# Third weight group issued ahead of the casts of the first, w_out's first third in two loads, leftover tokens of batches 0 and 1 joined to batch 2

## The chip, the cores and the metric

One core of one Trainium2 chip. The metric is the device time of one launch in microseconds (us); the median of several runs is quoted. The profile is one execution, and its span is some 2 us shorter than the time. TensorE (PE) does the matmuls, VectorE (DVE), ScalarE (ACT) and GpSimd (POOL) the rest; GpSimd also issues most loads.

## The reference, cut to what matters

```python
# attention without softmax: batch 8, heads 8, seq 576, head_dim 64
kv  = einsum('bhsd,bhse->bhde', k, v)
out = einsum('bhsd,bhde->bhse', q, kv)
x   = out / sqrt(mean(out*out, -1) + 1e-6) * g_norm       # then [4608 tokens, 512]
# gated feed-forward: d_model 512, d_ff 1536
ffn = (gelu(x @ w_gate) * (x @ w_val)) @ w_out
return x + sigmoid(x @ w_res) * ffn
```

Each batch has 576 tokens: 512 go into a block of the feed-forward, and the 64 left over of two batches make one tile of 128 for a ninth block at the end.

## The kernel before

The kernel is one long schedule. Blocks 0 to 7 hold 512 tokens each; while TensorE works on block n, the attention of batch n+1 is threaded in between. Only batch 0 has nothing to hide behind: its attention and the first matmuls of block 0 are an "opening", whose order on all engines is a list of words, read from left to right. A word is a piece of work on a pair of heads (digit), with the engine as the last letter where there is a choice: `vc3D` casts v of pair 3 on VectorE, `o2` multiplies q by kv, `sq`/`rd` square and reduce, `t2` scales, `xT2`/`xo2` transpose x and evict it, `g2`/`v2` are the matmuls with w_gate and w_val, `wcg0P`/`wcv0P` cast the first weight group on GpSimd, `w2` issues the loads of the third weight group.

```python
opening = """
... rt1 rd0 kc3A kvo2 qT3 w1 ri1 o2 rt0 t1 warm1 sq2 vc3D
rd2 qo3A xT1 kv3 wcg0P rt2 kvo3 ri0 ri2 warm2 o3 t2 xo1A wcg1P sq3a wcv0P sq3b xT2 t0 wcv1P rd3a xo2A g1
xT0 rd3b w2 v1 xo0D rt3 g2 gelu ri3 v2 t3a g0 t3b xT3a xT3b xo3aA xo3bD v0 w3 g3a v3a g3b v3b
"""
elif name == "w":              # 512 columns of w_gate, then of w_val, cast to fp16 by the DMA
    load_wg(pr)
    load_wv(pr)
...
# after the opening: w_res, batch 1, then w_out in thirds, all in the queue that GpSimd feeds
nc.gpsimd.dma_start(out=wr16, ...)
load_batch(1)
for f in range(0, NF, 4):
    load_wo(f, f + 4)
...
# leftover tokens of batches 0 and 1, threaded into block 1 on their own
at(1, 2, lambda: a_rem_qT(b))                  # 4 transposes on TensorE, 2 copies on ScalarE
at(1, 3, lambda: a_rem_o(b))                   # 8 matmuls
at(1, 8, lambda: a_norm(b, NJ, NJ + 1), t[NJ]) # 12 small VectorE instructions on 8 columns
at(1, NF + 1, x[NJ], lambda: a_x(b, NJ))       # 4 transposes on TensorE
...
pmoe  = ...tile_pool(name="pmoe",  bufs=4, space=PSUM)   # idle, o1, o0, then g and v tiles
pattn = ...tile_pool(name="pattn", bufs=4, space=PSUM)
```

Of the kernel before, what the change touches and what calls it, by code (L numbers as in the profile page):

```python
# [9 lines left out]
FP16 = mybir.dt.float16  # L10
# [8 lines left out]
def kernel(  # L19
# [15 lines left out]
    nc = tc.nc  # L35
# [6 lines left out]
    NJ = 4  # L42
# [80 lines left out]
    def load_wg(i):  # L123
        load_columns(wg_c, moe_w_gate, i)

    def load_wv(i):
        load_columns(wv_c, moe_w_val, i)
# [74 lines left out]
        a_ss(b, j, ps)  # L202
        s["o"][j] = ps

    def a_rem_qT(b):
        qr = qr_t[b // 2]
        ps = pattn.tile([P, NP, P], FP16, tag="at", name="qtrp")
        for pr in range(NP):
            nc.tensor.transpose(ps[:, pr, :], qr[:, pr * P : (pr + 1) * P], ident)
        nc.scalar.copy(out=qtr[0][:, :, 0:R], in_=ps[:, :, 0:R])  # L210
        nc.scalar.copy(out=qtr[1][:, :, R : 2 * R], in_=ps[:, :, R : 2 * R])

    def a_rem_o(b):
        ps = pattn.tile([P, C], FP32, tag="at", name="orp")
        for pr in range(NP):
            for e in range(2):
                nc.tensor.matmul(  # L217
                    ps[:, pr * P : (pr + 1) * P],
                    lhsT=qtr[e][:, pr, :],
                    rhs=st[b - 1 + e]["kv2"][:, pr, :],  # L220
                    start=(e == 0),
                    stop=(e == 1),
                )
        o32 = attnp.tile([P, C], FP32, tag="o32", name="o32")
        nc.scalar.copy(out=o32, in_=ps)
        a_ss(b, NJ, ps)
        st[b]["o"][NJ] = o32

    def a_norm(b, j0, j1):
# [14 lines left out]
        for _ in range(3):  # L244
            nc.vector.tensor_tensor(out=a, in0=yy, in1=yy, op=ALU.mult)
            nc.vector.tensor_tensor(out=a, in0=a, in1=mh, op=ALU.mult)
            nc.vector.scalar_tensor_tensor(out=yy, in0=a, scalar=1.5, in1=yy, op0=ALU.add, op1=ALU.mult)

    def where(b, j):
        return (b, j) if j < NJ else (B, b // 2)  # L250

    def a_t(b, j):

# [19 lines left out]
    def a_x(b, j):  # L273
        blk, jj = where(b, j)
        nc.vector.tensor_tensor(out=t_t[blk][:, jj, :], in0=t_t[blk][:, jj, :], in1=g16, op=ALU.mult)  # L275
# [8 lines left out]

    def d_rem_qT(b):
        st[b]["qrT"] = attnp.tile([P, NP, P], FP16, tag="qrT", name="qrT")
        nc.sync.dma_start(out=st[b]["qrT"], in_=qr_t[b // 2], transpose=True)

    def rem_qT_copy(b):
        nc.scalar.copy(out=qtr[0][:, :, 0:R], in_=st[b]["qrT"][:, :, 0:R])  # L290
# [324 lines left out]
    def f_piece(word):  # L615

        name = word.rstrip("0123abADP")
        rest = word[len(name) :]
        pr = int(rest[0])
        j0, j1 = {"a": (0, NJ // 2), "b": (NJ // 2, NJ)}.get(rest[1:2], (0, NJ))  # L620
        eng = rest[-1]
        if name in ("qc", "kc", "vc"):
            f_cast(name[0], pr, engines[eng])
        elif name in ("lk", "lv"):
            f_cast_last("kv".index(name[1]), pr, engines[eng])
        elif name == "warm":
            keep_warm(int(rest))
        elif name == "w":
            load_wg(pr)
            load_wv(pr)  # L630
        elif name in ("wcg", "wcv"):
            cs = slice(2 * pr, 2 * pr + 2)
            engines[eng](out=(wg_c if name == "wcg" else wv_c)[0][:, cs, :], in_=w_raw[name[-1]][:, cs, :])
        elif name == "qo":
            f_qT_out(pr, engines[eng])
        elif name in ("qT", "kv", "kvo", "o", "rt", "ri"):
            {"qT": f_qT, "kv": f_kv, "kvo": f_kv_out, "o": f_o, "rt": f_sqrt, "ri": f_rinv}[name](pr)
        elif name in ("sq", "rd", "t", "xT"):
            {"sq": f_sq, "rd": f_red, "t": f_t, "xT": f_xT}[name](pr, j0, j1)
        elif name == "xo":  # L640
            f_xT_out(pr, j0, j1, eng)
        elif name == "g":
            f_mm(wg_c, 0, pr, j0, j1)
        elif name == "v":
            f_mm(wv_c, 1, pr, j0, j1)
# [16 lines left out]

    opening = """
    qc1P qc0A qT1 qT0 kc1P kc0A qo0D warm3 lv0D lk0P qo1A warm3 vc1D vc0A kv1 qc2A kv0 kvo1 kvo0 o1 kc2P qT2
    lk1P lv1D sq1 qo2D o0 warm2 vc2P sq0 rd1 kv2 qc3P rt1 rd0 kc3A kvo2 qT3 w1 ri1 o2 rt0 t1 warm1 sq2 vc3D
    rd2 qo3A xT1 kv3 wcg0P rt2 kvo3 ri0 ri2 warm2 o3 t2 xo1A wcg1P sq3a wcv0P sq3b xT2 t0 wcv1P rd3a xo2A g1
    xT0 rd3b w2 v1 xo0D rt3 g2 gelu ri3 v2 t3a g0 t3b xT3a xT3b xo3aA xo3bD v0 w3 g3a v3a g3b v3b
    """

    def first_gval():  # L670
# [10 lines left out]
    def attn_plan_1():  # L681

        b = 1
        o = [lambda j=j: a_o(b, j) for j in range(NJ)]
        t = [lambda j=j: a_t(b, j) for j in range(NJ + 1)]
        x = [lambda j=j: a_xT(b, j) for j in range(NJ + 1)]
        plan = {
            NF - 1: [lambda: by_token(b, "q")],
            NF: [lambda: by_token(b, "k")],
            NF + 3: [  # L690
                lambda: attn_begin(b),
                lambda: a_qT(b, 0),
                lambda: a_qT(b, 1),
                lambda: load_batch(b + 1),
                lambda: a_kv(b, 0, NP),
            ],
            NF + 4: [o[0], o[1]],
            NF + 5: [o[2]],
            NF + 6: [o[3]],
            NF + 7: [lambda: a_norm(b, 0, NJ), t[0], t[1], t[2], t[3]],  # L700
            2 * NF + 1: [x[0], x[1]],
            2 * NF + 2: [x[2], x[3]],
        }

        at(1, 2, lambda: a_rem_qT(b))
        at(1, 3, lambda: a_rem_o(b))
        at(1, 8, lambda: a_norm(b, NJ, NJ + 1), t[NJ])
        at(1, NF + 1, x[NJ], lambda: a_x(b, NJ))
        return plan, [lambda j=j: a_x(b, j) for j in range(NJ)]

    plans = [{} for _ in range(B + 1)]
# [3 lines left out]
    def load_behind(b):  # L715

        nc.gpsimd.tensor_copy(out=hold, in_=st[b]["qT"][0:1, 0, 0, 0:1])  # L717
        if b % 2 == 1:
            nc.gpsimd.tensor_copy(out=hold, in_=st[b]["qrT"][0:1, 0, 0:1])
        load_batch(b + 1)  # L720

    def at(blk, slot, *fs):
        plans[blk].setdefault(slot, []).extend(fs)

    def plan_attn(b):


        odd = b % 2 == 1
        m = b - 1
        begin = [lambda: by_token(b, "k"), lambda: attn_begin(b), lambda: d_qT(b)]  # L730
        if odd:
            begin.append(lambda: d_rem_qT(b))
        if b == 2:
            at(m, 2, lambda: by_token(b, "q"))
            at(m, 3, *begin)
            k0, o0, n0 = 4, 6, 10
        else:
            at(m - 1, NF + 1, lambda: by_token(b, "q"))
            at(m - 1, NF + 2, *begin)
            k0, o0, n0 = 1, 3, 7  # L740
        at(m, k0, lambda: a_kv(b, 0, 2))
        at(m, k0 + 1, lambda: a_kv(b, 2, 4))
        if b + 1 < B:
            at(m, k0 + 1, lambda: load_behind(b))
        if odd:
            at(m, k0 + 1, lambda: rem_qT_copy(b))
            at(m, o0, lambda: a_rem_o(b))
        for j in range(NJ):
            at(m, o0 + j, lambda j=j: a_o(b, j))
        at(m, n0, lambda: a_norm(b, 0, NJ + b % 2))  # L750
        n0 += 1 if b == 2 else 2
        for j in range(NJ):
            at(m, n0 + j // 2, lambda j=j: a_t(b, j))
        if odd:
            at(m, n0 + 2, lambda: a_t(b, NJ))
        for j in range(NJ):
            at(m, NF, lambda j=j: a_x(b, j))
        at(m, NF, lambda: d_xT(b, 0, NJ))
        if odd:
            at(m, NF + 1, lambda: a_x(b, NJ), lambda: d_xT(b, NJ, NJ + 1))  # L760

    late = []
    for blk in range(B + 1):
        plan = plans[blk]
        if blk == 0:
            slots = [first_gval, None]
            slots += [lambda: m_gval(0, 2, pattn, "at")]
            slots += [lambda f=f: m_gval(0, f) for f in range(3, NF)]
            outs, stores = out_by_f(0)
            slots += outs  # L770
            for b in range(2, B):
                plan_attn(b)
            plan[5] = [lambda j=j: a_x(0, j) for j in range(NJ)]
        else:
            slots = [lambda f=f: m_gval(blk, f) for f in range(NF)]
            slots += [lambda j=j: m_out(blk, j) for j in range(NJ)]
            for j, fs in enumerate(late):
                plan.setdefault(j, []).extend(fs)
            late = []
# [7 lines left out]
        for s in range(len(slots)):  # L787
            if slots[s] is not None:
                slots[s]()
            for f in plan.pop(s, []):  # L790
                f()
            if blk == 0 and s == 2:
                nc.gpsimd.dma_start(out=wr16, in_=moe_w_res.rearrange("(cc p) c -> p cc c", p=P))
                load_batch(1)
                for f in range(0, NF, 4):
                    load_wo(f, f + 4)
        assert not plan
        if blk == 0:
            late = [[g] for g in stores] + [[] for _ in range(NJ)]
# [32 lines left out]
```

## Time and profile before

| | before |
|---|---|
| time, median | 355.73 us (355.16 to 356.32) |
| span of the profile, granted clock | 353.9 us, 1.000 |
| TensorE busy | 343.9 us, 1874 matmuls |
| opening ends (first matmul of block 0's third group) | 20.84 us |
| first output matmul (fps) | 45.75 us |
| last matmuls start | 346.79 us |

The share of busy time (97%) says little, as it averages a start that waits for data and a long rest that does not. The chain that ended last, by engine, says which is which:

```profile
PE 84%; DMA 11%; DVE 2%; SPq 1%; POOL 1%; issue 1%; ACT 0%; DVEq 0%
```

11% of 353.9 us, about 39 us, are transfers: the chain runs through loads up to 45.7 us and through TensorE from there.

### The profile page before, as it was taken

The page shows a single profiled execution, that of the slowest core. Times are in us where ns is not written, and L with a number is a line of the kernel's source. Part 1 is how long each engine was busy: PE and PEld are TensorE (multiplying, and loading weights), DVE is VectorE, ACT ScalarE, POOL GpSimd, SP SyncE. Part 2 cuts the span into 40 slices and gives each one's busy share as a digit, 9 for nine tenths or more (in the row PEclk, how much of TensorE's full clock was granted, in tenths as well). Part 3 has the DMA queues.
Part 4 walks back from the last instruction along what each step waited for, and adds up shares of the span by engine and source line. Part 5 has one row for each costly group of instructions (what it writes and reads, how often), then busy time and mean ns, then how long its engine had stood idle before and what let it go on. Part 6 is the DMA issues. An engine that isn't in the chain of part 4 may idle for free.

```text
span 353.9 us, 4990 instructions
## 1 busy us (share of the span) xinstructions
PE 343.9 (97%) x1874; PEld 167.9 (47%) x1874; DVE 217.4 (61%) x445; ACT 125.3 (35%) x216; POOL 49.5 (14%) x77
## 2 busy tenths in 40 slices
PE   8799989999999999999999999999999999999995
PEld 3544544554454445444554445444544444444443
DVE  6855357879748774776569556965587533334433
ACT  3653624452245222532263124322642233223320
POOL 2782410050050005000410022000000000000000
PEclk9999999999999999999999999999999999999999
DMA  8999999597799078904690469226000500020013
GB/s 245 308 174 202 197 202 114 180 144 66 182 154 120 0 151 162 142 0 119 156 179 0 107 151 183 17 69 183 2 0 32 145 17 2 31 89 2 1 30 89
DMA packets 77242, 38.46 MB, mean 109 GB/s; under 512 B 41250, under 2 KB 72738, under 8 KB 77218
## 3 DMA queue, kind: packets, MB, share of 16 engines
q0 software_dynamic: 38736, 17.17, 38.5%
q1 hardware_dynamic: 38320, 20.85, 21.9%
q8 instruction: 14, 0.23, 0.3%
q10 hardware_dynamic: 162, 0.13, 0.1%
q14 instruction: 10, 0.08, 0.1%
HBM read 38.80 MB, written 9.44 MB: 136 GB/s over the span
## 4 chain that ended last, share of the span: by engine, by line
PE 84%; DMA 11%; DVE 2%; SPq 1%; POOL 1%; issue 1%; ACT 0%; DVEq 0%
PE fps L352 25%; PE gps L319 23%; PE vps L319 23%; PE rps L339 8%; DMA wo<-in_moe_w_out_dram 5%; DMA wg<-in_moe_w_gate_dram 3%; PE op L199 2%; DMA kf<-in_k_dram 2%; DMA wvf<-in_moe_w_val_dram 2%; PE kvp L169 2%; PE fps L381 1%; DVE hid L308 1%; SPq L433 1%; PE orp L217 1%; PE kvp L177 0%
## 5 line engine op out<-in xcount | busy, mean ns | idle before, releaser
L308 DVE TENSOR_TENSOR hid<-ge,vps 128x512 f16<-128x512 f16 x108 | 73.4, 685 | 64.3 <-PE vps L319 58.0
L319 PE MATMUL gps<-xT,wg 128*128 128x512 f16 x424 | 108.8, 379 | 0.3 <-ACT xT L269 0.3
L319 PE MATMUL vps<-xT,wv 128*128 128x512 f16 x424 | 108.8, 379 | 0.0
L307 ACT ACTIVATE ge<-gps 128x512 f16<-128x512 f32 x108 | 64.5, 598 | 112.9 <-PE gps L319 104.1
L352 PE MATMUL fps<-wo,hid 128*128 128x512 f16 x420 | 96.9, 379 | 2.2 <-DMA wo<-in_moe_w_out_dram 1.9
L319 PEld LDWEIGHTS <-wv 128*128 128x128 f16 x424 | 41.4, 98 | 50.2 <-DMA wv<-in_moe_w_val_dram 0.5
L352 PEld LDWEIGHTS <-hid 128*128 128x128 f16 x420 | 40.8, 98 | 50.9 <-DMA wo<-in_moe_w_out_dram 2.1
L319 PEld LDWEIGHTS <-wg 128*128 128x128 f16 x424 | 39.9, 98 | 41.3 <-DVE pf L358 0.6
L358 DVE SCALAR_TENSOR_TENSOR pf<-th,fps 128x512 f32<-128x512 f32 x35 | 23.8, 686 | 48.0 <-PE fps L352 48.0
L348 ACT ACTIVATE th<-rps 128x512 f32<-128x512 f32 x36 | 21.5, 598 | 77.3 <-PE rps L339 77.3
L339 PE MATMUL rps<-wr,xT 128*128 128x512 f16 x144 | 36.5, 379 | 0.0
L193 DVE TENSOR_REDUCE ss<-sq 128x8 f32<-128x512 f32 x32 | 21.5, 683 | 7.6 <-ACT sq L192 5.8
L363 DVE SCALAR_TENSOR_TENSOR osb<-pf,t 128x512 f32<-128x512 f32 x35 | 24.2, 691 | 1.1
L339 PEld LDWEIGHTS <-xT 128*128 128x128 f16 x144 | 14.0, 98 | 16.6
L192 ACT ACTIVATE sq<-op 128x512 f32<-128x512 f32 x28 | 16.6, 598 | 12.6 <-PE op L199 11.9
L717 POOL COPY hold<-qT 1x1 f16<-1x1 f16 x5 | 0.9, 179 | 138.0 <-DMA qT<-q 138.0
L256 DVE TENSOR_TENSOR t<-op,ny 128x512 f16<-128x512 f32 x28 | 17.8, 680 | 0.1
L275 DVE TENSOR_TENSOR t<-t,g 128x512 f16<-128x512 f16 x36 | 13.3, 417 | 0.0
L169 PE MATMUL kvp<-v,k 128*128 128x128 f16 x128 | 10.9, 222 | 0.8 <-POOL v L522 0.7
L169 PEld LDWEIGHTS <-k 128*128 128x128 f16 x128 | 9.3, 99 | 4.8 <-issue 1.8
L199 PEld LDWEIGHTS <-qT 128*128 128x128 f16 x112 | 8.4, 98 | 5.7
L199 PE MATMUL op<-kv,qT 128*128 128x128 f16 x112 | 10.7, 219 | 0.0
(107 smaller groups left out, 182.4 us busy)
## 6 DMA issues: line engine op xcount, KB each, us to landing
out_dram<-osb SPq DMA_DIRECT2D x32, 256.0 KB, 2.3
qraw<-in_q_dram POOLq DMA_DIRECT2D x7, 512.0 KB, 6.0
kraw<-in_k_dram POOLq DMA_DIRECT2D x7, 512.0 KB, 7.9
v<-in_v_dram POOLq DMA_DIRECT2D x7, 512.0 KB, 9.9
wo<-in_moe_w_out_dram POOLq DMA_DIRECT2D x3, 512.0 KB, 17.0
wg<-in_moe_w_gate_dram POOLq DMA_DIRECT2D x2, 512.0 KB, 7.3
wv<-in_moe_w_val_dram POOLq DMA_DIRECT2D x2, 512.0 KB, 9.1
out_dram<-osb SPq DMA_DIRECT2D x6, 128.0 KB, 2.3
```

The costliest lines, as they stand in the source:

```text
L169: nc.tensor.matmul(ps, lhsT=k16[:, j, cs], rhs=v16[:, 2 * pr : 2 * pr + 2, j * D : (j + 1) * D], start=(j == 0), stop=False,)
L193: nc.vector.tensor_reduce(out=st[b]["ss"][:, j, :], in_=sq, op=ALU.add, axis=mybir.AxisListType.X)
L199: nc.tensor.matmul(ps[:, pr * P : (pr + 1) * P], lhsT=s["qT"][:, j, pr, :], rhs=s["kv2"][:, pr, :], start=True, stop=True)
L256: nc.vector.tensor_tensor(out=t_t[blk][:, jj, :].rearrange("p (h d) -> p h d", h=H), in0=s["o"][j].rearrange("p (h d) -> p h d", h=H), in1 ...
L307: nc.scalar.activation(out=ge, in_=gps, func=AF.Gelu)
L308: nc.vector.tensor_tensor(out=hids[blk][:, f, :], in0=ge, in1=vps, op=ALU.mult)
L319: nc.tensor.matmul(ps[:, j0 * P : j1 * P], lhsT=w[:, cc, :], rhs=xT_t[blk][:, j0:j1, cc, :], start=(cc == 0 and j0 == 0), stop=(cc == NP - ...
L339: nc.tensor.matmul(rps, lhsT=xT_t[blk][:, j, cc, :], rhs=wr16[:, cc, :], start=(cc == 0), stop=(cc == NP - 1),)
L348: nc.scalar.activation(out=th, in_=rps, func=AF.Tanh, scale=0.5)
L352: nc.tensor.matmul(fps, lhsT=hids[blk][:, f, j * P : (j + 1) * P], rhs=wo16[:, f, :], start=(f == 0), stop=(f == NF - 1))
L358: nc.vector.scalar_tensor_tensor(out=pf, in0=th, scalar=1.0, in1=fps, op0=ALU.add, op1=ALU.mult)
L363: nc.vector.scalar_tensor_tensor(out=osb, in0=pf, scalar=0.5, in1=t_t[blk][:, j, :], op0=ALU.mult, op1=ALU.add)
```

## The change

Its intent: close a hole in the stream of weights, let TensorE start on half of w_out's first third, and take the leftover tokens of batches 0 and 1 off TensorE's own transposes. Cut to its core (small helper edits that follow from it are left out):

```diff
-    def a_rem_qT(b): ...            # transposes of the leftover q on TensorE
-                    rhs=st[b - 1 + e]["kv2"][:, pr, :],
+                    rhs=st[2 * pair(b) + e]["kv2"][:, pr, :],
+    def pair(b):                    # which pair of batches is finished with batch b
+        return b // 2 if b % 2 == 1 and b > 1 else 0 if b == 2 else None
-        elif name == "w":
+        elif name == "wg":
             load_wg(pr)
+        elif name == "wv":
             load_wv(pr)
-    ... rt1 rd0 kc3A kvo2 qT3 w1 ri1 o2 ... vc3D
-    rd2 qo3A xT1 kv3 wcg0P rt2 kvo3 ri0 ri2 warm2 o3 t2 xo1A wcg1P sq3a wcv0P sq3b xT2 t0 wcv1P rd3a xo2A g1
-    xT0 rd3b w2 v1 xo0D rt3 g2 gelu ri3 v2 t3a g0 t3b xT3a xT3b xo3aA xo3bD v0 w3 g3a v3a g3b v3b
+    ... rt1 kvo2 rd0 kc3A qT3 wg1 wv1 ri1 o2 ... vc3D
+    rd2 qo3A xT1 kv3 wg2 wcg0P rt2 kvo3 ri0 ri2 warm2 o3 t2 xo1A wcg1P sq3a wv2 wcv0P sq3b g1 xT2 rd3a wcv1P rd3b
+    t0 xo2A wg3 wv3 v1 xT0 rt3 ri3 xo0A g2 v2 t3a t3b xT3a g0 xT3b xo3aA xo3bD gelu v0 g3a v3a g3b v3b
-        at(1, 2, lambda: a_rem_qT(b)) ... at(1, NF + 1, x[NJ], ...)   # batch 1's own leftover pass
-        odd = b % 2 == 1
+        rem = pair(b) is not None   # batches 2, 3, 5, 7 carry a leftover tile, transposed by DMA
+            if blk == 1:
+                slots[0] = lambda: m_gval(1, 0, pattn, "at")
-                for f in range(0, NF, 4):
-                    load_wo(f, f + 4)
+                for f0, f1 in ((0, 2), (2, 4), (4, 8), (8, NF)):
+                    load_wo(f0, f1)
```

More of the change, by code (lines that the diff above doesn't have):

```diff
@@ L203, in a_o @@
         s["o"][j] = ps
-    def a_rem_qT(b):
-        qr = qr_t[b // 2]
-        ps = pattn.tile([P, NP, P], FP16, tag="at", name="qtrp")
-        for pr in range(NP):
-            nc.tensor.transpose(ps[:, pr, :], qr[:, pr * P : (pr + 1) * P], ident)
-        nc.scalar.copy(out=qtr[0][:, :, 0:R], in_=ps[:, :, 0:R])
-        nc.scalar.copy(out=qtr[1][:, :, R : 2 * R], in_=ps[:, :, R : 2 * R])
     def a_rem_o(b):
@@ L247, in a_norm @@
             nc.vector.scalar_tensor_tensor(out=yy, in0=a, scalar=1.5, in1=yy, op0=ALU.add, op1=ALU.mult)
+    def pair(b):
+        return b // 2 if b % 2 == 1 and b > 1 else 0 if b == 2 else None
     def where(b, j):
-        return (b, j) if j < NJ else (B, b // 2)
+        return (b, j) if j < NJ else (B, pair(b))
     def a_t(b, j):
@@ L286, in d_rem_qT @@
         st[b]["qrT"] = attnp.tile([P, NP, P], FP16, tag="qrT", name="qrT")
-        nc.sync.dma_start(out=st[b]["qrT"], in_=qr_t[b // 2], transpose=True)
+        nc.sync.dma_start(out=st[b]["qrT"], in_=qr_t[pair(b)], transpose=True)
     def rem_qT_copy(b):
@@ L664 @@
     qc1P qc0A qT1 qT0 kc1P kc0A qo0D warm3 lv0D lk0P qo1A warm3 vc1D vc0A kv1 qc2A kv0 kvo1 kvo0 o1 kc2P qT2
-    lk1P lv1D sq1 qo2D o0 warm2 vc2P sq0 rd1 kv2 qc3P rt1 rd0 kc3A kvo2 qT3 w1 ri1 o2 rt0 t1 warm1 sq2 vc3D
-    rd2 qo3A xT1 kv3 wcg0P rt2 kvo3 ri0 ri2 warm2 o3 t2 xo1A wcg1P sq3a wcv0P sq3b xT2 t0 wcv1P rd3a xo2A g1
-    xT0 rd3b w2 v1 xo0D rt3 g2 gelu ri3 v2 t3a g0 t3b xT3a xT3b xo3aA xo3bD v0 w3 g3a v3a g3b v3b
+    lk1P lv1D sq1 qo2D o0 warm2 vc2P sq0 rd1 kv2 qc3P rt1 kvo2 rd0 kc3A qT3 wg1 wv1 ri1 o2 rt0 t1 warm1 sq2 vc3D
+    rd2 qo3A xT1 kv3 wg2 wcg0P rt2 kvo3 ri0 ri2 warm2 o3 t2 xo1A wcg1P sq3a wv2 wcv0P sq3b g1 xT2 rd3a wcv1P rd3b
+    t0 xo2A wg3 wv3 v1 xT0 rt3 ri3 xo0A g2 v2 t3a t3b xT3a g0 xT3b xo3aA xo3bD gelu v0 g3a v3a g3b v3b
     """
@@ L684, in attn_plan_1 @@
         o = [lambda j=j: a_o(b, j) for j in range(NJ)]
-        t = [lambda j=j: a_t(b, j) for j in range(NJ + 1)]
-        x = [lambda j=j: a_xT(b, j) for j in range(NJ + 1)]
+        t = [lambda j=j: a_t(b, j) for j in range(NJ)]
+        x = [lambda j=j: a_xT(b, j) for j in range(NJ)]
         plan = {
@@ L703, in attn_plan_1 @@
         }
-        at(1, 2, lambda: a_rem_qT(b))
-        at(1, 3, lambda: a_rem_o(b))
-        at(1, 8, lambda: a_norm(b, NJ, NJ + 1), t[NJ])
-        at(1, NF + 1, x[NJ], lambda: a_x(b, NJ))
         return plan, [lambda j=j: a_x(b, j) for j in range(NJ)]
@@ L717, in load_behind @@
         nc.gpsimd.tensor_copy(out=hold, in_=st[b]["qT"][0:1, 0, 0, 0:1])
-        if b % 2 == 1:
+        if pair(b) is not None:
             nc.gpsimd.tensor_copy(out=hold, in_=st[b]["qrT"][0:1, 0, 0:1])
@@ L725, in plan_attn @@
     def plan_attn(b):
-        odd = b % 2 == 1
+        rem = pair(b) is not None
         m = b - 1
         begin = [lambda: by_token(b, "k"), lambda: attn_begin(b), lambda: d_qT(b)]
-        if odd:
+        if rem:
             begin.append(lambda: d_rem_qT(b))
@@ L744, in plan_attn @@
             at(m, k0 + 1, lambda: load_behind(b))
-        if odd:
+        if rem:
             at(m, k0 + 1, lambda: rem_qT_copy(b))
@@ L749, in plan_attn @@
             at(m, o0 + j, lambda j=j: a_o(b, j))
-        at(m, n0, lambda: a_norm(b, 0, NJ + b % 2))
+        at(m, n0, lambda: a_norm(b, 0, NJ + rem))
         n0 += 1 if b == 2 else 2
@@ L753, in plan_attn @@
             at(m, n0 + j // 2, lambda j=j: a_t(b, j))
-        if odd:
+        if rem:
             at(m, n0 + 2, lambda: a_t(b, NJ))
@@ L758, in plan_attn @@
         at(m, NF, lambda: d_xT(b, 0, NJ))
-        if odd:
+        if rem:
             at(m, NF + 1, lambda: a_x(b, NJ), lambda: d_xT(b, NJ, NJ + 1))
```

## The prediction

> **What bounds the kernel now.** I read the busy table first, then the waits of TensorE, then the chain of waits, then the DMA rate in one-microsecond windows over the opening, and last the timeline around each wait.
>
> ```profile
> PE 343.9 (97%) x1874; PEld 167.9 (47%) x1874; DVE 217.4 (61%) x445; ACT 125.3 (35%) x216; POOL 49.5 (14%) x77
> PE fps L352 <- DMA wo<-in_moe_w_out_dram: 1.9, 1, 1.9
> PE fps L352 <- DVE hid L308: 0.3, 1, 0.3
> PE gps L319 <- ACT xT L269: 0.3, 1, 0.3
> 25.28 0.55 PEld L319 LDWEIGHTS <-wv 128*128 128x128 f16 x4 [0.45 <-DMA wv<-in_moe_w_val_dram]
> 45.75 0.55 PEld L352 LDWEIGHTS <-hid 128*128 128x128 f16 x4 [2.05 <-DMA wo<-in_moe_w_out_dram]
> 28.12 17.58 DMA wo<-in_moe_w_out_dram
> ```
>
> The first line says that TensorE is busy 97% of 353.9 us at the full granted clock, so ten microseconds of idle time are all there is beside its work. The next ones say where the idle time lies that this change can reach: one wait of 1.9 us for the first third of w_out before the first output matmul (the chain shows it issued at 28.12 and landed 17.58 later, at 45.70), 0.45 us at 25.28 for the third group of w_val, 0.3 us for VectorE at the end of block 1 and 0.3 us for ScalarE at the start of block 1. After 60 us nothing else stalls TensorE: every window of 30 us from 90 to 330 us shows it busy for all of it. So whatever arrives earlier in the first 45 us shifts the whole rest of the kernel to the left, one for one, and after that only TensorE work itself counts.
>
> ```profile
> core 0: us, PE busy (x) PEld busy (x) DVE busy (x) ACT busy (x) POOL busy (x), PEclk, DMA share, GB/s
> 17.00:18.00 1.00, 1.00 (x9) 0.59 (x8) 1.00 (x4) 0.90 (x2) 1.00 (x3) 1.00 1.44 196
> 18.00:19.00 1.00, 1.00 (x7) 0.47 (x5) 0.96 (x4) 0.98 (x2) 1.00 (x2) 1.00 0.53 63
> 19.00:20.00 1.00, 0.98 (x9) 0.46 (x8) 0.42 (x2) 0.82 (x2) 1.00 (x2) 1.00 0.78 94
> 20.00:21.00 1.00, 1.00 (x9) 0.84 (x9) 0.00 (x0) 0.29 (x1) 1.00 (x3) 1.00 1.20 197
> ```
>
> ```profile
> 17.23 0.74 POOL L121 DMA_DIRECT2D wg<-in_moe_w_gate_dram  x1
> 17.96 0.75 POOL L121 DMA_DIRECT2D wv<-in_moe_w_val_dram  x1
> ```
>
> The last column is what the DMA engines write. From 16 to 45 us it stands at about 200 GB/s (fp16 written, so about 400 GB/s of fp32 read) except here: at 18 to 20 us it drops to 63 and 94. The second weight group (issued at 12.66 and 13.56, landing 4.8 and 5.2 us later, that is at 17.5 and 18.8) has run out, and the third was issued only at 17.23, because the GpSimd program has the four casts of the first group ahead of it. The hole is worth (200-63)/200 + (200-94)/200 = 1.2 us of transfer time, and the one queue behind it (groups three and four, w_res, batch 1, w_out) never catches up: it is full until after 58 us.
>
> **What the Trainium skill says.** "DMA: Bandwidth & Descriptors", section "Specifications", gives a fabric ceiling of 435 GB/s for a core's 16 engines; the 400 GB/s read side here is close under it, so I take the queue as bound by rate. The same page, "Anatomy of one DMA — SWDGE (gpsimd) path", puts about 2 us of fixed cost on each such transfer; the trace agrees: from the issue at 17.23 to full flow at about 20 us is 2.8 us. Issues must therefore run that far ahead. "Perfetto Trace Analysis", section "DMA Optimizations", says that splitting may let some chunks start sooner, above all where DMA engines are idle; here they are not idle, so a split moves the landing of the first half and nothing else. "TensorE: Matmul & The Clock Gate", section "Wait — 56ns, not 53.3ns?", gives 55.6 and 215.7 ns from one warm matmul to the next at 128 and 512 columns; the chain agrees (8 transposes in 0.45 us, 4 matmuls in 0.86 us).
>
> **The change part by part.** (a) The third group of w_gate goes out before the first cast and that of w_val between the casts. GpSimd is free at 14.33 and idles until 14.83 for the first raw group. So w_gate goes out at 14.33, 2.9 us earlier, and w_val at about 16.3 (14.33 + 0.75 issue + two casts of 0.62, end to end), 1.7 us earlier. Both are behind the second group in the queue and fill the hole. All later landings move about 1.2 us forward: w_val's third group from about 25.26 to 24.1, which takes away the 0.45 us wait, and the first third of w_out from 45.70 to 44.5.
>
> (b) That third is split. A half is 256 KB at 200 GB/s = 1.3 us, so its first half should land near 44.5 - 1.3 = 43.2. The second half comes at 44.5. TensorE needs it only after two steps and most of an attention piece, 0.86 + 0.45 + 0.86 + 0.22 = 2.4 us later. The other two thirds (about 47.1 and 49.7) are also ahead of their use. The GpSimd queue seems to hold eight transfers in flight (the three w_out issues each waited for the transfer eight earlier), so one more transfer pushes the last third's issue behind the landing of batch 1's q at about 35; there is slack for it.
>
> (c) The opening's order. The two casts of w_val are now behind one 0.75 us issue: the first ends at about 17.65 instead of 16.74, so the first w_val matmuls, which ran at 17.41, start at 17.7. From there TensorE has five pairs of matmuls (v1, g2, v2, g0, v0) at 2 x 0.216 = 0.43 each, the eight half-width matmuls of the last pair (0.86) and two sets of four transposes (0.22 each), in all 2.15 + 0.86 + 0.44 = 3.45 us: end at about 21.15 instead of 20.84. The reordering on VectorE (mask of pair 2 ahead of one reduction, pair 3's reductions ahead of pair 0's scaling, one 0.47 us eviction given to ScalarE) works in the other direction by 0.1 to 0.4 us on pair 3's chain, but that chain isn't then the last. I take +0.3 us, uncertain by 0.4. The later table load on ScalarE (1.28 us) is not in TensorE's way, as the next user of a buffer freed by the first GELU comes two matmul groups later.
>
> So TensorE would be ready for the output matmuls at 43.87 - 0.45 + 0.3 = 43.7, and their weights are there at 43.2. Start at about 43.8 instead of 45.75: **2.0 us**.
>
> (d) The leftover tokens of batches 0 and 1 go with batch 2. Eight transposes on TensorE (four of q at 63.5, four of x at 89.1), with their ScalarE evictions, become two DMA transposes: **0.45 us** of TensorE in a stretch where it is the bound. The eight matmuls of orp stay. The separate norm on eight columns (twelve instructions from 77.76 to 79.97, 2.2 us of VectorE) disappears, since the joined one has 40 columns in place of 32 at the same 0.19 us each. That VectorE time is what made the last hid of block 1 late, so the wait of **0.3 us** at 85.45 should go too.
>
> (e) Block 1's first pair of matmul groups takes other PSUM buffers. The weight load there waited 0.63 us for pf, but the matmul itself started at 58.34, when the last xT eviction ended (58.30). That operand wait stays: nothing gained.
>
> Sum: 2.0 + 0.45 + 0.3 = 2.75; I take 2.5 for what will not fit together so well, and 355.73 - 2.5 = 353.2.
>
> **The rivals.** First: the queue doesn't get faster by the earlier issue, because the second group would share the engines with the third or because the raw groups on the hardware queue (until 16 us) take the rate. For it: the rate before 16 us is already 360 to 390 GB/s. Against it: the hole lies after those transfers. Then only the split counts: start at 44.4, 1.3 us, and with 0.75 of block 1 the time is 353.7. Second: the opening becomes longer by more than I reckon (POOL issues ahead of casts, VectorE has under 0.1 us idle between 11.8 and 17.5 us) and TensorE reaches the output matmuls at 44.5 with its weights there: also 1.2 us, 353.8; a wait at one place only becomes a wait at another. Third: the joined work delays block 1, as ScalarE has to wait for the transposed leftover q ahead of a GELU, or the attention of batch 2 for its q transpose. Against it: the transpose is issued at about 66 and lands some 4 us later, the copy comes two slots (about 4 us) after it. It would cost up to 1 us: 354.2. Fourth: the opening gains as well (pair 3's chain really is the last), which gives 352.7.
>
> **The range.** The floor is all waits gone plus the transposes: 1.9 + 0.45 + 0.45 + 0.3 = 3.1 and a little from the opening, 352.3. The upper end is the first two rivals together with run spread (the three runs before lie within 1.2 us): 354.6. Two per cent is 7.1 us, more than twice all idle time that the change can reach; a loss of 7 us would need a stall that nothing here suggests. So within 2% is nearly sure.
>
> **What would show it.** In the changed profile: the one-microsecond windows at 18 to 20 us at about 200 GB/s; no wait at the w_val weight load near 25 us; the first output matmul at 43.5 to 44.2, with a wait for w_out under 0.5 us; the end of the opening's matmuls at 20.8 to 21.4; 1866 matmuls; no wait for hid at the end of block 1; from there on the same work shifted. I am wrong if the first output matmul starts after 44.7, if the opening ends after 21.6 or before 20.5, or if block 1 shows a new wait.

## The result, and the profile after

The changed kernel took 353.43 us (353.16 to 353.84, 4 runs), the one before 355.75 us in the same rounds: ratio 0.9936, 95% interval 0.9917 to 0.9955. A ratio is the mean time of one kernel's fast runs over that of the other's of the same rounds, so it is not quite the ratio of the medians. The gain of 0.6% is clear of the noise and below the 2% at which the record calls a kernel faster. The forecast was 353.2 us.

The busy row and the chain by engine of the changed kernel, then TensorE's waits (us in total, times, longest):

```profile
PE 343.2 (98%) x1866; PEld 167.5 (48%) x1866; DVE 215.3 (61%) x432; ACT 124.9 (36%) x216; POOL 50.3 (14%) x79
PE 92%; DMA 3%; POOL 2%; DVE 1%; ACT 0%; issue 0%; SPq 0%; DVEq 0%
```

```profile
PE vps L603 <- POOL wv L630: 0.5, 1, 0.5
PE gps L315 <- ACT xT L265: 0.3, 1, 0.3
PE gps L603 <- POOL wg L630: 0.2, 1, 0.2
```

The transfers' share of the chain went from 11 to 3%. The waits for w_out and for hid are gone. A wait of 0.5 us stands in the opening instead, before the first matmuls with w_val. The DMA rate in one-microsecond windows (last column), where 63 and 94 stood:

```profile
17.00:18.00 1.00, 0.51 (x3) 0.21 (x3) 0.84 (x3) 0.88 (x2) 1.00 (x3) 1.00 1.46 199
18.00:19.00 1.00, 1.00 (x9) 0.56 (x8) 0.90 (x3) 0.49 (x1) 1.00 (x3) 1.00 1.29 207
19.00:20.00 1.00, 1.00 (x9) 0.57 (x8) 0.04 (x1) 0.69 (x3) 1.00 (x2) 1.00 1.24 207
20.00:21.00 1.00, 1.00 (x9) 0.77 (x8) 0.35 (x1) 1.00 (x1) 1.00 (x2) 1.00 1.24 211
```

And the two landmarks on TensorE's timeline (start, duration), the end of the opening and the first output matmul, which has no wait beside it any more:

```profile
21.13 1.03 PE L315 MATMUL gps<-xT,wg 128*128 128x512 f16 x4
...
43.86 1.03 PE L348 MATMUL fps<-wo,hid 128*128 128x512 f16 x4
```

The last matmuls start at 344.35, 2.44 us earlier than before.

**A ruler for single profiles.** The profiles of one kernel differ by over 2 us in when the opening ends (21.13 and 23.52 in two of the changed kernel), 1.5 us of it because the first loads of k and v do not land at the same moment in each run. So I cut each profile at four marks: the arrival of v (the start of GpSimd's cast of v, `vc2P`; in after2, norem and pool it follows the cast of k without a wait, so there a late k sets it), the end of the opening, the first output matmul and the last matmuls. The three distances between them leave out the moment of the arrival. For the two profiles above: 9.39, 24.91 and 301.04 us before, 9.72, 22.73 and 300.49 us after. The differences, +0.33, -2.18 and -0.55, and 0.04 us of arrival make the 2.44.

### The profile page after: what moved, and what is told of

It reads as the page before. It is cut to its first block, busy times and chain, and to the rows that moved or that the text cites. A ratio compares the mean times of both kernels' runs of the same rounds, so it can differ in the third digit from the quotient of the medians.

```text
span 351.4 us, 4970 instructions
## 1 busy us (share of the span) xinstructions
PE 343.2 (98%) x1866; PEld 167.5 (48%) x1866; DVE 215.3 (61%) x432; ACT 124.9 (36%) x216; POOL 50.3 (14%) x79
## 4 chain that ended last, share of the span: by engine, by line
PE 92%; DMA 3%; POOL 2%; DVE 1%; ACT 0%; issue 0%; SPq 0%; DVEq 0%
PE gps L315 26%; PE vps L315 26%; PE fps L348 26%; PE rps L335 9%; PE kvp L169 2%; PE op L199 2%; DMA vf<-in_v_dram 1%; DMA kf<-in_k_dram 1%; PE fps L377 1%; PE vps L603 1%; PE orp L209 1%; POOL wg L121 0%; PE kvp L177 0%; POOL wv L121 0%; PE gps L603 0%; ACT xT L265 0%
```

## The experiments

All runs gave results that agree with the reference. Times of one call share the runs of the kernel before (355.89, 355.91 and 355.76 us median in the three calls). "Early" is the third weight group ahead of the casts; "split" the two loads of w_out's first third; "joined" the leftover tokens with batch 2.

| kernel | early | split | joined | opening's new order | median us | ratio to before (95%) | arrival to opening's end | to first output matmul | to last matmuls |
|---|---|---|---|---|---|---|---|---|---|
| before | - | - | - | - | 355.75 | 1 | 9.39 | 24.91 | 301.04 |
| before, again (before2) | - | - | - | - | (one look) | | 10.22, half clock | 23.56 | 301.03 |
| split_only | - | x | - | - | 354.68 | 0.9966 (0.9946 to 0.9985) | 9.40 | 23.98 | 301.11 |
| rem_only | - | - | x | - | 355.38 | 0.9983 (0.9961 to 1.0005) | 9.39 | 24.31 | 300.42 |
| early_only | x | - | - | - | 354.55 | 0.9976 (0.9952 to 0.9999) | 9.60 | 22.86 | 301.04 |
| late_nosplit | - | - | x | x | 354.90 | 0.9973 (0.9954 to 0.9993) | 10.49, half clock | 23.16 | 300.42 |
| late | - | x | x | x | 354.62 | 0.9961 (0.9945 to 0.9978) | 9.72 | 23.69 | 300.49 |
| nosplit | x | - | x | x | 353.66 | 0.9938 (0.9921 to 0.9955) | 9.72 | 22.75 | 300.46 |
| norem | x | x | - | x | 354.82 | 0.9976 (0.9960 to 0.9993) | (slow profile) | 22.73 | 301.11 |
| changed | x | x | x | x | 353.43 | 0.9936 (0.9917 to 0.9955) | 9.72 | 22.73 | 300.49 |
| changed, again (after2) | x | x | x | x | 353.90 | 0.9953 (0.9933 to 0.9974) | 10.57, half clock | 22.73 | 300.49 |

The kernels of the first call are nosplit, late, late_nosplit and rem_only; after2, early_only, norem and fix are of the second, split_only, fix_xt, pool and before2 of the third.

My theory: the stream of weights is bound by its rate, and the hole at 18 to 20 us makes all that follows 1.2 us late; filling it is the gain. The rivals: the split is the gain; the new order of the opening is; the PSUM pool is.

### Without the split (nosplit)

```diff
-for f0, f1 in ((0, 2), (2, 4), (4, 8), (8, NF)):
+for f0, f1 in ((0, 4), (4, 8), (8, NF)):
```

> The changed kernel with the first third of w_out in one load again. In the changed kernel both halves had landed (42.3 and 43.7 us) before TensorE was ready for them (43.86), so theory A (the earlier issue of the third weight group alone takes the w_out wait away, the split is spare): first output matmul at 43.9, wait under 0.2 us, time within 0.3 us of the changed kernel (353.4). Rival B (one large load lands later than two halves[...]; before, it took 3.7 us after the load ahead of it and not 2.6): it lands at 44.4 to 44.7, wait 0.5 to 0.9 us, time about 354.1.

Measured: 353.66 us, between the two medians of the changed kernel (353.43 and 353.90). The landing of the whole third (us from issue), and the first output matmul, which does not wait:

```profile
wo<-in_moe_w_out_dram POOLq DMA_DIRECT2D x1, 512.0 KB, 16.2
...
44.61 1.04 PE L348 MATMUL fps<-wo,hid 128*128 128x512 f16 x4
```

The whole third, issued at 28.39, landed 16.2 us later, at 44.59. That is 32.45 us after the arrival of v, and TensorE is ready 9.72 + 22.73 = 32.45 us after it: the landing meets the need to within 0.1 us. The split is a margin here (in the changed kernel the first half landed at 42.3 and the second at 43.7, TensorE came at 43.86), not a gain. Theory A holds, rival B falls.

The margin is used in some runs. In the profiles of after2 and pool, where the cast of v started only at 12.95 and 13.26 us, the rate dropped again to 106 and 78 GB/s between 19 and 20 us, although the third w_gate load had been issued at 15.68 and 16.11. This is pool:

```profile
19.00:20.00 1.00, 0.60 (x3) 0.25 (x4) 0.83 (x3) 0.82 (x2) 1.00 (x3) 1.00 1.16 78
```

Why it dropped there is not shown. In pool the second half landed at 46.21 and TensorE started on the first at 45.73, so one load would have cost an estimated 0.5 us in that run.

### Third group late again (late), and late without the split (late_nosplit)

```diff
-kv3 wg2 wcg0P ... sq3a wv2 wcv0P ... t0 xo2A wg3 wv3 v1
+kv3 wcg0P ... sq3a wcv0P ... t0 xo2A wg2 wv2 wg3 wv3 v1
```

> The changed kernel with the third weight group issued behind the four casts again, split kept. The hole in the transfers at 18 to 20 us comes back, so does the 0.45 us wait for w_val near 25 us, and the wait of 0.49 us for the w_val cast in the opening goes (opening ends at 20.6 to 20.9). Theory A (queue bound by rate, landing 1.2 us later in all): first half of w_out at about 43.5, before TensorE is ready at 43.9, so no w_out wait, 353.3 to 353.6. Rival B (the split alone buys only the 1.3 us of half a load): first half at 44.4, wait 0.5 us, 353.9 to 354.1.

> The changed kernel with both undone: third group behind the casts, w_out's first third in one load. The wait for w_out comes back at 1.7 to 2.1 us and only the leftover tokens (0.75 us: 8 transposes 0.45, late hid 0.3) and the opening's order remain: 354.9 to 355.2. If the opening's new order or the PSUM pool of block 1 were the real gain, it would stay near 353.5.

Measured: 354.62 and 354.90 us. So the early issue is worth 1.2 us without the split (354.90 - 353.66) and about 0.7 to 1.2 us with it (against the changed kernel's two medians, 353.90 and 353.43). The split, with the group late, is worth 0.3 us by the medians of these two kernels, which is inside the spread. In the windows of late the hole is back (86 GB/s at 18 to 20 us), and with it a wait for w_val, larger than before:

```profile
18.00:20.00 2.00, 1.75 (x13) 1.02 (x13) 1.15 (x4) 1.15 (x4) 2.00 (x4) 1.00 0.70 86
```

```profile
26.78 1.04 PE L315 MATMUL vps<-xT,wv 128*128 128x512 f16 x4 [0.79 <-DMA wv<-in_moe_w_val_dram]
```

I expected 353.3 to 353.6 for late and missed by a microsecond: I had this wait at 0.45 us as in the first profile, and I had the opening at 20.6 to 20.9 us, 0.3 us shorter, with the w_val load out of the way of its cast. It is not shorter: 9.72 us, as in the changed kernel. So the load between the casts is not what made the opening longer. The timeline of late shows what did, with no load near it:

```profile
18.25 0.38 PE L603 MATMUL vps<-xT,wv 128*128 128x512 f16 x1 [0.62 <-DVE t L577]
```

The second w_val matmul waits for `t0` on VectorE. In the changed kernel, too, it started as `t0` ended: `t0` ran until 17.82, and of the pair of matmuls that ran from 17.53 to 18.25 the second, 0.38 long, began at about 17.87.

```profile
17.14 0.68 DVE L577 TENSOR_TENSOR t<-op,rinv 128x512 f16<-128x512 f32 x1
```

The matmul does not read what `t0` writes. What they share, by the order in which the code takes buffers, is a PSUM buffer: the four of that pool go in turn to idle, o1, o0, the two g tiles and the two v tiles, so the second v tile gets the one in which o of pair 0 lies until `t0` has read it. The new order puts `t0` behind two reductions of pair 3. The wait is shown; that the shared buffer is its reason is read from the code, and no run moved `t0` alone. In late_nosplit the time was at the lower edge of what was expected, but the w_out wait of 1.7 to 2.1 us was not there: it was 0.27 us, as this profile has a stretch of half clock in the opening (below) that uses up the time.

### The joined leftover tokens alone (rem_only), and the changed kernel without them (norem)

```diff
 # rem_only: the kernel before, with of the change only
+    def pair(b): ...        # and its uses, the pass of its own for batches 0 and 1 taken out
 # norem: the kernel before with all of the change but this
```

> The kernel before with the leftover tokens of batches 0 and 1 joined to batch 2, nothing else. Expected: 1866 matmuls, no wait for hid at the end of block 1, last matmuls 0.75 us earlier than before: 355.0. Rival: VectorE's slack is taken by something else in block 1 and only the 0.45 us of transposes is saved: 355.3.

> The changed kernel with the leftover tokens of batches 0 and 1 as before (own transposes on TensorE, own norm). Expected 0.45 us of transposes plus a late hid of 0 to 0.3 us at the end of block 1: 0.45 to 0.75 us over the changed kernel of this call. Rival: under 0.2 us, if block 1 has slack that the joined norm uses up.

Measured: 355.38 us for rem_only, nearer to its rival's 355.3 than to 355.0, ratio 0.9983 with an interval that reaches 1; norem is 0.9976 beside 0.9953 for the changed kernel of the same call, so 0.0023 of 355.9, or 0.8 us, again with wide intervals. (The profile of norem fell in the slow state; its other six runs are fast, and only they count in the ratio. Its marks after the opening are used in the table, as the granted clock is full from 28 us on.) The last column of the table is sharper: from the first output matmul to the last it is 301.04 against 300.42 us (before, rem_only) and 301.11 against 300.49 (norem or split_only, changed): 0.62 us both times. The expected 0.75 was the sum of 0.45 and 0.3. What happened: the transposes went (0.45), and the stall for hid went, which measured at the next matmul's start was 0.48 us (the 12 matmuls from 82.60 need 2.59 us, the next group started at 85.67 instead of 85.19), but a new wait came. The stall in the profile of before, then the new wait in the changed kernel's:

```profile
85.45 0.39 PE L352 MATMUL fps<-wo,hid 128*128 128x512 f16 x1 [0.31 <-DVE hid L308]
```

In block 1, TensorE now reaches the attention of batch 2 earlier than VectorE has sorted its k:

```profile
64.28 1.03 PE L315 MATMUL vps<-xT,wv 128*128 128x512 f16 x4
64.70 0.68 DVE L107 COPY k<-kraw 128x2048 f16<-128x2048 f16 x1
65.31 0.68 DVE L359 SCALAR_TENSOR_TENSOR osb<-pf,t 128x512 f32<-128x512 f32 x1
65.44 0.23 PEld L169 LDWEIGHTS <-k 128*128 128x128 f16 x4 [0.63 <-DVE k L107]
```

Four matmuls take 4 x 0.216 = 0.86 us, so TensorE could have gone on at 65.14 and went on at 65.45: 0.31 us. 0.45 + 0.48 - 0.31 = 0.62. The waits of the matmul rows do not list it, as it is put down to the weight load. The same wait of 0.63 us stands in the profile of rem_only, and none in that of before.

### The early issue alone (early_only)

```diff
-... qT3 w1 ri1 ... kv3 wcg0P ... sq3a wcv0P ... rd3b w2 v1 ... v0 w3 g3a
+... qT3 wg1 wv1 ri1 ... kv3 wg2 wcg0P ... sq3a wv2 wcv0P ... rd3b wg3 wv3 v1 ... v0 g3a
```

> The kernel before with one thing changed: the third weight group issued ahead of the casts (w_gate) and between them (w_val). Theory A (queue bound by rate; the early issue fills the hole and by itself moves the first third of w_out up to the time it is needed): no wait for w_val near 25 us, w_out wait under 0.3 us, the opening 0.3 to 0.5 us longer by the wait for the w_val cast; 1.3 to 1.9 us less than before, 354.0 to 354.5. Rival: the early issue needs the split or the new opening order to count; then a w_out wait of 0.7 us or more stays, and 355 us.

Measured: 354.55 us, 1.3 us under before by the medians (0.9976, so 0.9 us, by the means, in which one run of 356.63 counts), just above the 354.0 to 354.5 that were expected. The wait for w_val is gone, and the first output matmul starts 22.86 us after the opening, 0.13 over the floor of 22.73. The opening is 0.21 us longer than before, less than the 0.3 to 0.5 expected, and here it is the load between the casts that does it: `t0` stands where it stood, and the weight load of the first w_val matmul waits 0.18 us for the cast. So the early issue needs neither the split nor the new order.

The landing of w_out's first third, counted from the arrival of v, shows the 1.2 us of the theory: 33.7 us in rem_only (issued at 28.94, landed 16.3 later, v at 11.56), 33.6 in late_nosplit and 33.8 in the second profile of before; 32.4 in early_only and 32.5 in nosplit. The first profile of before had 34.3, half a microsecond later than its like: there the third landed 3.7 us after the load ahead of it, in the others 2.5 to 2.6 us after it.

### The split alone (split_only)

```diff
-for f in range(0, NF, 4):
-    load_wo(f, f + 4)
+for f0, f1 in ((0, 2), (2, 4), (4, 8), (8, NF)):
+    load_wo(f0, f1)
```

> The kernel before with w_out's first third in two loads, nothing else. Theory A (the queue is late as a whole, so the split only lets TensorE start on half a third): the w_out wait shrinks from 0.3 to 1.9 us to below 0.5, the wait for w_val near 25 us stays at 0.4 to 0.8 us; 0.4 to 1.2 us under before, 354.7 to 355.4. Rival (the split is the main part of the gain): 354.2 or less.

Measured: 354.68 us, 0.9966 (0.9946 to 0.9985), 1.1 to 1.2 us under before. The w_out wait is gone: the first half landed 32.6 us after v and was not needed before 9.40 + 22.73 = 32.1 us plus the wait for w_val, which is 1.1 us here, more than the 0.4 to 0.8 expected. What the split is worth when it is alone is less sure than these times say: from the arrival of v to the first output matmul it is 33.38 us here (9.40 + 23.98), against 33.70 in rem_only, 33.78 in before2 and 34.30 in the first profile of before, so 0.3 to 0.9 us; early_only has 32.46. Early and split remove the same wait for w_out, but only the early issue removes the one for w_val as well. With both (nosplit against the changed kernel) the split adds nothing in these marks: the gains do not add up. The rival (354.2 or less) falls.

### The same kernels once more (before2, after2)

No edit.

> The kernel before, one more profile, to see how far the waits for w_val and w_out of one kernel move from run to run. Expected: their sum between 1.2 and 2.4 us (2.3 in the first profile), the hole at 18 to 20 us below 110 GB/s, block 1's wait for hid 0.3 us.

> The changed kernel once more, on one chip with the three below. The first profiles differ by up to 0.7 us in when the opening ends, with the same instructions up to there, so single profiles of one kernel have to be compared. Expected: 353.2 to 353.7 us, opening end 20.8 to 21.9, both halves of w_out landed before the first output matmul, no w_out wait in this profile either.

Measured: one profile of before at 355.71 us and six runs of the changed kernel, 353.39 to 355.51. Their median, 353.90 us, and the end of the opening in the profile, 23.52 us, are outside what I expected. Both profiles have a stretch in the opening in which TensorE's granted clock is half (the third number from the end of a window's line):

```profile
16.00:18.00 2.00, 1.99 (x11) 1.07 (x10) 1.97 (x7) 1.33 (x4) 1.88 (x4) 0.50 1.44 202
```

This is before2. Summed over its windows from 14 to 20 us, the clock was half for 0.88 + 2.0 + 0.56 = 3.4 us, if it is either full or half. Its opening is 0.83 us longer (10.22), and yet the first output matmul starts at the same time as in the first profile, 45.73 against 45.75; only the wait is smaller:

```profile
45.73 1.04 PE L352 MATMUL fps<-wo,hid 128*128 128x512 f16 x4 [0.40 <-DMA wo<-in_moe_w_out_dram]
```

So before, the moment is set by the transfers, and a late opening is hidden. In the changed kernel it is not: in after2 the opening took 10.57 us, and the first output matmul came 22.73 us later without any wait:

```profile
23.52 1.03 PE L315 MATMUL gps<-xT,wg 128*128 128x512 f16 x4
...
46.25 1.03 PE L348 MATMUL fps<-wo,hid 128*128 128x512 f16 x4
```

The times point the same way. The seven fast runs of the changed kernel with a mean clock of 0.997 or more took 353.44 us on average, the three at 0.995 354.78. That is not the clock alone: of the 2.4 us by which after2's first output matmul is later than in the first profile, the longer opening is 0.85 us and the later arrival of v 1.54 us. A run of pool with the clock at 1.000 took 354.99 us, with v at 13.26. The kernel before took 355.82 us (23 runs) at 0.997 or more and 355.88 us (10 runs) at 0.993 to 0.995, no difference. I had expected the waits of before2 to sum to 1.2 us or more (they were 0.4 and 0.6): the first profile's 2.3 us is not a constant of the kernel, it is what the transfers leave over of an opening of 9.39 us.

### w_val's third load behind its casts (fix)

```diff
-sq3a wv2 wcv0P sq3b ... rd3b
-t0 xo2A wg3 wv3
+sq3a wcv0P sq3b ... rd3b
+t0 wv2 xo2A wg3 wv3
```

> The changed kernel with the third group of w_val issued after the two w_val casts, w_gate's third group still first. Theory: the queue has 2.6 us of w_gate to move by then, so no hole opens (18 to 20 us at 200 GB/s), and the 0.49 us wait for the w_val cast in the opening shrinks to below 0.1; the opening ends 0.25 us earlier (then scaled pair 0 is the last), time 0.2 to 0.3 us under the changed kernel. Rival: the hole comes back in part (under 180 GB/s between 18 and 20 us) and what is won in the opening is lost near 25 us as a wait for w_val.

Measured: 353.60 us, 0.9941 (0.9926 to 0.9956), beside 0.9953 (0.9933 to 0.9974) for the changed kernel of the same call; the intervals overlap, and its marks are those of the changed kernel's first profile, 9.72, 22.73 and 300.49. No hole opened (203 GB/s), so that rival falls, but nothing was won: the wait for the cast turned into the wait for `t0`.

```profile
18.39 0.38 PE L603 MATMUL vps<-xT,wv 128*128 128x512 f16 x1 [0.62 <-DVE t L577]
```

### One eviction of x on VectorE (fix_xt)

```diff
 def a_xT(b, j):
+    if j == 1:
+        nc.vector.tensor_scalar(out=xT_t[blk][:, jj], in0=ps, scalar1=gcol, scalar2=None, op0=ALU.mult)
+    else:
         nc.scalar.activation(out=xT_t[blk][:, jj], in_=ps, func=AF.Copy, scale=gcol)
```

> The version with w_val's third group behind the casts, and in addition one of the four evictions of x of batch 1 on VectorE (0.47 us, idle there) in place of ScalarE (0.65 us). Expected: the 0.27 us wait of block 1's first matmul for the last ScalarE eviction is gone, 0.2 to 0.3 us under the version without it (ratio to before 0.9941): 353.1 to 353.3 in runs whose clock is 0.997 or above. Rival: VectorE gets to it late, behind the scaling of batch 1's last tile, and the wait is only renamed.

Measured: 354.09 us, 0.9956 (0.9931 to 0.9981); three of its six runs had a clock of 0.995, the others took 353.50 to 353.86. The marks are those of fix. A miss: the wait is as long as it was.

```profile
54.83 0.48 DVE L266 TENSOR_SCALAR xT<-xtp,gcol 128x512 f16<-128x512 f16 x1
55.91 1.26 ACT L268 ACTIVATE xT<-xtp,gcol 128x512 f16<-128x512 f16 x2 [0.62 <-PE xtp L264]
57.23 1.02 PE L318 MATMUL gps<-xT,wg 128*128 128x512 f16 x4 [0.27 <-ACT xT L268]
```

VectorE evicts tile 1 in good time, but ScalarE then idles 0.62 us until TensorE has transposed tiles 2 and 3 and evicts both one after the other. One of these two would have had to go over; that was not run.

### The PSUM pool of block 1's first pair (pool)

```diff
-            if blk == 1:
-                slots[0] = lambda: m_gval(1, 0, pattn, "at")
```

> The changed kernel with block 1's first pair of matmul groups back in the PSUM buffers of the other groups. Expected: no difference (within 0.1 us of the changed kernel in runs at a clock of 0.997 or above, 353.2 to 353.9): the matmul waits 0.27 us for the last xT eviction either way. Rival: the wait for pf (0.63 us at the weight load before) delays the start by 0.2 to 0.4 us more.

Measured: 354.19 us, 0.9948 (0.9928 to 0.9969); three of the four runs at a clock of 0.997 or more are in the expected range, the profiled one (354.99, late arrival of v) is not. Marks 9.74, 22.73 and 300.49, as in the changed kernel. The weight load's wait for pf is back (0.63 us) and costs nothing, as the matmul waits for the eviction anyway:

```profile
58.38 1.02 PE L315 MATMUL gps<-xT,wg 128*128 128x512 f16 x4 [0.27 <-ACT xT L265]
```

## Why the prediction was right

The total was right (353.2 against 353.43 us, 2.5 against 2.3 us saved), and most steps hold; two of them, the split and the opening, were right in sum and not in the reason.

- **The hole and what it is worth.** Right. The windows stand at 199 to 211 GB/s in the first profile of the changed kernel (not in every later one: 106 in after2); with the third group early, w_out's first third lands 1.2 us earlier after the arrival of v (32.4 and 32.5 against 33.6 to 33.8).
- **When the output matmuls start.** 43.8 was forecast, 43.86 measured, and the wait for w_val went. (In after2 it is 46.25: the forecast's absolute times hold for loads that arrive as in the first profile.)
- **What the split is worth.** The step that took the landing of the whole third at 44.5 us, so 0.8 us too late for a TensorE ready at 43.7, and had the split bring it under the need, was mis-sized. It was built on the first profile's landing of 45.70, which is half a microsecond later than in the other profiles of kernels with the late group. In the changed kernel the whole third had landed at 43.7. So the split gained nothing in that profile; where the group is late it gained 0.3 us (late against late_nosplit) to 1.1 us (split_only against before), a spread that these runs do not narrow. The rival in which only the split counts fell.
- **The opening.** +0.3 was forecast, +0.33 measured: luck, as the reason was wrong. The wait it named, for the w_val cast, does stand in the changed profile (0.49 us), but without it nothing is won. The load between the casts does cost 0.21 us where the order is the old one (early_only), but in the new order late has the same 9.72 us without any load between its casts. The step "pair 3's chain isn't then the last" overlooked that the second w_val matmul waits for `t0`, by the code for its PSUM buffer.
- **The leftover tokens.** 0.75 was forecast, 0.62 measured: 0.45 as reckoned, the hid stall 0.48 instead of 0.3, and a new wait of 0.31 for k on VectorE, the kind that the third rival named, on another operand. A new wait in block 1 was one of the prediction's own signs of being wrong; it took back 0.31 of the 0.93 us. The wait of ScalarE for the leftover q that the rival named came too (1.04 us, at 68.72), with no wait on TensorE after it.
- **The pool.** Zero, as forecast.
- **The spread.** The range covers it, but not for its reason. The changed kernel has moved from being bound by transfers to being bound by TensorE in its first 46 us, and so it now shows a stretch of half clock in the opening (0.85 us in after2), which the one before hides.
- **A reading that does not carry.** The 2.8 us from the issue at 17.23 to full flow do not confirm the 2 us of fixed cost: "DMA: Bandwidth & Descriptors", section "Anatomy of one DMA — SWDGE (gpsimd) path", puts most of that cost after the last byte. In quarter-microsecond windows the rate is back above 40 GB/s at 18.75 us, 1.5 us after the issue, and at 188 from 20.0 on. No step of the sum rests on it. And the rate outside the hole is not 200 everywhere: from 40 to 41 us it is 164.

Left open: why the clock is halved in some runs of the same program; why the rate drops again where the first loads arrive late; and whether `t0` ahead of pair 3's reductions (an estimated 0.1 us, 9.72 against the 9.60 of early_only, or 0.3 us with w_val's load behind its casts, against 9.40) and the attention of batch 2 one slot later in block 1 (an estimated 0.3 us, the wait for k) would add to the gain. No version was run that clearly beats the changed kernel.

## What to carry to other kernels

Two remedies for one wait need not add up: measure each alone and both together before both are kept as gains. Where a kernel starts bound by a queue of transfers, look for windows in which the rate drops, as the time lost there comes back in every later landing, and check what the next bound is, since from then on its jitter is yours. And an instruction that is put later on an engine with slack can still hold a buffer that another engine waits for.

## What the Trainium skill lacked or had wrong

- "TensorE: Matmul & The Clock Gate", section "What's actually happening", gives two clock states, the lower one at half, and a window of about 3.4 us. The runs agree: half the granted clock, for 3.4 us in before2. It also says that the slow start varies between runs of one kernel. What it does not have is that a stretch after the start can be slow in some runs of a program and not in others: in before2 the clock is full up to 15 us, half up to about 18.6 and full again, in the first profile of the same kernel it is full throughout, both with matmuls put in to keep the array busy. In after2, which has such a stretch, the opening took 0.85 us longer.
- "Perfetto Trace Analysis", section "DMA Optimizations", recommends splitting where DMA engines are idle. Here they were busy and the split alone still gained something (354.68 against 355.76 us; 0.3 us in late against late_nosplit), since a consumer that works through the load in order can start on half; with the landing already moved up it gained nothing that can be told from the spread.
- "DMA: Bandwidth & Descriptors", section "Specifications", has a ceiling that this case stays under (about 400 of 435 GB/s on the reading side, worked out from 200 written). No page has how far the landing of first loads moves from run to run: the cast of v, which waits for v or for the cast of a late k, started between 11.41 and 13.26 us in fast profiles of programs that are the same up to there or nearly so.
